# Padding a selector to 128 columns, moving three blocks of work in time, and changing an eviction ratio in a one-core training-step kernel

## The chip, the cores and the metric

The kernel runs on one core of one Trainium2 chip. The metric is device microseconds (us) of one execution; a "median" is that of several executions, and the "span" is that of the one execution that was profiled. All runs quoted here are of the fast state, that is, none shows the longer time at a lower clock that some executions have. Engine names in the profile: PE is TensorE (matmuls), PEld its weight loads, DVE VectorE, ACT ScalarE, POOL GpSimd, SP SyncE. An "eviction" here is a copy of a finished PSUM tile to SBUF.

## The reference

The kernel computes a transformer block with adaptive layernorm and the gradient of all its inputs. S = 2048, D = 512, 32 heads of 16, F = 1792, bf16. What matters of the forward part:

```python
def _A_ref(x, wqkv, wo):            # H = 32, Dh = 16, W = 8, dil = 2
    qkv = (x @ wqkv) ...            # -> q, k, v
    idx = pos[:, None] - off[None, :]          # off = 0, 2, .., 14
    logits = einsum('bhsd,bhswd->bhsw', q, kg) * scale   # 8 shifted keys a query
    attn = softmax(where(mask, logits, -1e9))
    return (einsum('bhsw,bhswd->bhsd', attn, vg)) ... @ wo

h = layernorm(x) * (1 + ca) + sa
x = x + ga * _A_ref(h, A_wqkv, A_wo)
h = layernorm(x) * (1 + cb) + sb
x = x + gb * ((h @ w_gate) * (h @ w_up)) @ w_down
# (sa, ca, ga, sb, cb, gb) = silu(c) @ w_mod
# the result is x and the gradients of 8 inputs for a given grad_out
```

## The kernel before

It is one long program of stages; a library places waits and hands out buffers from pools. Each pool tile is named by a tag, and a tag has a fixed number of buffers. Five places matter.

Logits: q times a shifted k on VectorE, then a 64-column selector matmul on TensorE sums over each head's 16 rows. The projection matmuls of the next head tile come between.

```python
Gsel = const.tile([P, W, 8 * W], BF16, name="Gsel")        # 64 columns
psA, psB, psT: PSUM pools of 2, 4 and 2 buffers

def logits_ht(ht):
    htpair, htlo = divmod(ht, 2)
    for sc in range(NCH):
        lt_ps = ps_tile(psA, "lt_ps")
        for w in range(W):
            prod = wt(0, "prodL")
            ew.mul(prod[:], qT[...], kT[... shifted by DIL * w ...])
            nc.tensor.matmul(lt_ps[htlo * 64:(htlo + 1) * 64, :], lhsT=Gsel[:, w, :], rhs=prod[:], start=(w == 0), stop=(w == W - 1))
        evac(LT_sb[htlo * 64:...], lt_ps[htlo * 64:...])
for ht in range(DC):
    qkv_proj(0 * DC + ht); qkv_proj(1 * DC + ht)     # q and k
    if ht >= 1: logits_ht(ht - 1)
for ht in range(DC):
    qkv_proj(2 * DC + ht)                            # v
    if ht == 0: logits_ht(DC - 1)
# ... softmax; attn_tok is carved from the big buffer tag BIG1, as W1 and h1T are
```

FFN output: 56 transposes of Wd (its copy is stored for the backward part) stand ahead of the matmuls.

```python
for fc in range(FC):                                 # FC = 14
    for dc in range(DC):
        nc.tensor.transpose(out=stgw[:, dc, :], in_=Wd[:, fc, ...], identity=ident[:])
    evac(wTt[:], stgw[:], eng="v"); store(WdT_d[...], wTt[:])
```

Attention backward, "the accumulation stage", 128 steps (4 head tiles x 4 chunks x 8 shifts):

```python
evac.set_ratio(3, 1)       # of each 4 evictions, 3 on ScalarE and the 4th on VectorE
for w in range(W):
    nc.tensor.matmul(arep_ps[:], lhsT=RepSel[...], rhs=attnT2[...])     # 2 buffers for
    evac(arep_sb[:], arep_ps[:])                                        # arep and
    nc.tensor.matmul(dlrep_ps[:], lhsT=RepSel[...], rhs=dlT[...])       # dlrep together
    evac(dlrep_sb[:], dlrep_ps[:])
    ew.mul(Y, arep_sb, d_oT);    shifted_acc(dv_ps, ..., Y, w)          # VectorE, TensorE
    ew.mul(Pq, dlrep_sb, kT2);   nc.tensor.matmul(dq_ps[:], lhsT=ident, rhs=Pq)
    ew.mul(Pk, dlrep_sb, qT2);   shifted_acc(dk_ps, ..., Pk, w)         # Pk: tag wb4
```

The end: the weight gradient dwqkv (48 steps of 4 transposes, an eviction and 4 matmuls), then 16 tiles of layernorm backward, then the gradient of c.

```python
for fq in range(3):
    for t in range(NT):
        ... 4 transposes, evac(stg_sb, stg, eng="v"), 4 matmuls into dwq_acc
for t in range(NT):
    x_l = wt(4, "x_l9");  load(x_l[:], x_dram[:, t, :])        # tag wb4
    ... 12 matmuls dh1_ps, then ln_bwd_tile: n_bwd (ACT), dn (DVE, ACT), qq (DVE, ACT),
        negm, Aq (DVE), Bq (ACT), dx (DVE), prodca (DVE), dca_ps (PE)
for n in (0, 1): dwmod_chunk(n)
for dc in range(DC):                       # 4 multiply-reduces of 3072 columns
    nc.vector.tensor_tensor_reduce(out=junk10, in0=wmod2[:, dc, :], in1=dmod_rep, ...)
nc.sync.dma_start(out=out_7.rearrange("o (dc p) -> p (o dc)", p=P), in_=dc_bf[:])   # 1 KB
```

## Time and profile before

| | before |
|---|---|
| median of 15 runs | 1367.41 us (1365.33 to 1371.49) |
| profiled span | 1366.9 us |
| granted TensorE clock, mean | 0.921 |
| busy share PE / DVE / ACT | 82 / 62 / 37% |

The page's first two parts: busy time of each engine, then the busy tenths in 40 equal slices of the span (here the rows of three engines and of the granted clock).

```profile
span 1366.9 us, 16522 instructions
PE 1118.5 (82%) x5743; PEld 508.6 (37%) x5828; DVE 851.5 (62%) x2291; ACT 501.2 (37%) x939; POOL 117.3 (9%) x226
...
PE   3799499759989788979997888869768888899860
...
DVE  6567799984446654763444223234979999954465
ACT  2333467513321111454445010012036666643471
...
PEclk9699699869999899989997999989889999999985
```

No engine binds the whole. The rows must be read slice by slice (34 us each): PE is at 9 in slices 3 and 4 (the logits), DVE at 9 from slice 31 to 35 (the accumulation stage), and in the last slice PE is at 0.

The view of windows shows the same by stage: window, its length, then busy us of each engine with the number of instructions, then granted clock, DMA share and GB/s.

```profile
core 0: us, PE busy (x) PEld busy (x) DVE busy (x) ACT busy (x) POOL busy (x), PEclk, DMA share, GB/s
57.00:141.00 84.00, 82.89 (x292) 25.98 (x296) 50.43 (x128) 33.63 (x59) 1.06 (x2) 0.99 0.12 51
141.00:170.00 29.00, 10.45 (x67) 5.94 (x68) 25.58 (x81) 11.74 (x23) 1.06 (x2) 0.54 0.27 105
397.00:467.00 70.00, 60.57 (x308) 27.73 (x312) 43.93 (x120) 8.37 (x17) 19.36 (x32) 0.98 0.37 115
1019.00:1209.00 190.00, 166.39 (x813) 68.95 (x813) 178.99 (x463) 122.99 (x222) 0.00 (x0) 0.99 0.05 10
1209.00:1367.00 158.00, 108.98 (x600) 51.32 (x610) 75.34 (x180) 64.33 (x135) 12.85 (x21) 0.87 0.24 86
```

Logits: PE is busy 82.9 of 84 us. But busy is not the same as fast: the timeline of PE (start, duration, line, operation) has three consecutive starts there.

```profile
86.04 0.40 PE L359 MATMUL lt_ps<-prodL,Gsel 128*64 128x512 bf16 x1
86.38 0.39 PE L345 MATMUL qkv_ps<-big_p 128*128 128x512 bf16 x1
86.70 0.40 PE L359 MATMUL lt_ps<-prodL,Gsel 128*64 128x512 bf16 x1
```

The starts are 0.34 and 0.32 us apart where the weight is 64 columns wide in one matmul and 128 in the next. Between two projection matmuls they are about 0.22 apart, between two selectors 0.24. The timeline of the weight loads (PEld) shows what is lost: at each change of width the load starts together with its own matmul (86.04 and 86.38, as above), after the matmul before it has been issued.

```profile
86.04 0.11 PEld L359 LDWEIGHTS <-Gsel 128*64 128x64 bf16 x1 [0.23 <-issue]
86.38 0.10 PEld L345 LDWEIGHTS <-big_p 128*128 128x128 bf16 x1 [0.23 <-issue]
```

So it is, within about 5 ns, at all but one of the 167 changes of width between the first and the last logits matmul; between neighbours of one width the load mostly starts 0.21 us ahead or more, under the matmul before.

The accumulation stage: VectorE is busy 179 of 190 us, and the view of groups shows what it does beside multiplying (busy us, mean ns of one, then idle time before it). A ScalarE eviction of the same tile is a little shorter, 598 against 681 ns.

```profile
L62 DVE CAST dlrep_sb<-dlrep_ps 128x512 bf16<-128x512 f32 x64 | 43.6, 681 | 0.2 <-PE dlrep_ps L803 0.2
L60 ACT ACTIVATE dlrep_sb<-dlrep_ps 128x512 bf16<-128x512 f32 x64 | 38.3, 598 | 29.0 <-PE dlrep_ps L803 26.2 <-DVE Pq L84 1.4 <-DVE Yv L84 0.9
```

The end: the timeline has the last of four multiply-reduces and then a small store; the view of DMA issues gives the store's size and the us from issue to landing.

```profile
1347.88 3.36 DVE L888 CUSTOM_DVE_ANT_0 m_p<-big_p,m_p 128x3072 bf16<-128x3072 bf16 x1
...
1351.68 0.39 SPq L899 DMA_DIRECT2D out_dram<-dc_bf  x1
```
```profile
out_dram<-dc_bf SPq DMA_DIRECT2D x1, 1.0 KB, 14.1
```

The kernel ends when one kilobyte has landed, 14.1 us after it was issued, with every engine idle.

### The profile page before, as it was taken

How to read it: one execution, taken by the hardware profiler on the slowest of the kernel's cores; microseconds unless marked ns; L12 is line 12 of the kernel's file. 1: busy time of each engine (PE TensorE's matmuls, PEld its weight loads, DVE VectorE, ACT ScalarE, POOL GpSimd, SP SyncE). 2: the span in 40 equal slices, each digit the busy share in tenths (PEclk: the TensorE clock that was granted, in tenths of full speed). 3: DMA queues.
4: the chain of work that ended last, by engine and by line, in shares of the span. 5: the costliest groups of instructions: out<-in, count | busy, mean ns of one | idle time of the engine just before them, and what ended most of it. 6: DMA issues, size and time to landing. Idle time of an engine off the chain costs nothing. (4 is left out here: it accounts for less than half of the span.)

```text
span 1366.9 us, 16522 instructions
## 1 busy us (share of the span) xinstructions
PE 1118.5 (82%) x5743; PEld 508.6 (37%) x5828; DVE 851.5 (62%) x2291; ACT 501.2 (37%) x939; POOL 117.3 (9%) x226
## 2 busy tenths in 40 slices
PE   3799499759989788979997888869768888899860
PEld 1332233324444244434442455444233333345420
DVE  6567799984446654763444223234979999954465
ACT  2333467513321111454445010012036666643471
POOL 2000000221122311001111000000000000000010
PEclk9699699869999899989997999989889999999985
DMA  6111200542243420122323005050101000041121
GB/s 215 47 63 63 100 9 1 218 129 75 65 127 97 153 78 28 51 104 82 97 85 140 34 31 211 16 162 4 43 17 31 1 1 0 1 177 58 62 67 38
DMA packets 62691, 101.94 MB, mean 75 GB/s; under 512 B 29712, under 2 KB 50448, under 8 KB 60560
## 3 DMA queue, kind: packets, MB, share of 16 engines
q1 hardware_dynamic: 50400, 56.21, 12.7%
q0 software_dynamic: 12208, 44.67, 8.8%
q8 instruction: 45, 0.74, 0.2%
q14 instruction: 38, 0.31, 0.1%
HBM read 54.10 MB, written 44.66 MB: 72 GB/s over the span
## 5 line engine op out<-in xcount | busy, mean ns | idle before, releaser
L62 DVE COPY stg_sb<-stg 128x512 bf16<-128x512 bf16 (+1 forms) x248 | 90.0, 401 | 209.7 <-PE stg L666 102.4
L671 PE MATMUL dw_acc<-stg_sb,m_h2tok 128*128 128x512 bf16 (+1 forms) x497 | 108.4, 356 | 20.7 <-DVE stg_sb L62 17.9
L60 ACT ACTIVATE arep_sb<-arep_ps 128x512 bf16<-128x512 f32 x128 | 76.5, 597 | 33.1 <-PE arep_ps L799 32.8
L671 PEld LDWEIGHTS <-m_h2tok 128*128 128x128 bf16 x512 | 49.6, 98 | 68.6 <-issue 27.1
L84 DVE TENSOR_TENSOR prodL<-big_qkv 128x512 bf16<-128x512 bf16 x128 | 50.4, 423 | 36.3 <-PE lt_ps L359 29.8
L62 DVE CAST big_u<-gu_ps 128x512 bf16<-128x512 f32 x56 | 38.7, 691 | 51.3 <-PE gu_ps L477 51.3
L550 PE MATMUL dwd_ps<-m_dffn,stg_sb 128*128 128x512 bf16 x215 | 54.1, 390 | 14.8 <-DVE stg_sb L62 14.2
L803 PE MATMUL dlrep_ps<-m_p,RepSel 128*128 128x512 bf16 x128 | 48.7, 381 | 19.0 <-ACT dlrep_sb L60 10.6
L60 ACT ACTIVATE dw_sb<-dw_acc 128x512 bf16<-128x512 f32 (+1 forms) x32 | 14.8, 550 | 133.5 <-issue 116.3
L345 PE MATMUL qkv_ps<-big_p 128*128 128x512 bf16 x184 | 60.0, 414 | 3.4 <-DVE big_p L62 1.9
L627 PE MATMUL dh_ps<-m_wgT,big_u 128*128 128x512 bf16 x218 | 55.4, 393 | 7.3 <-DMA m_wgT<-WgT_d 6.9
L60 ACT ACTIVATE big_g<-gu_ps 128x512 bf16<-128x512 f32 x56 | 33.4, 597 | 74.7 <-PE gu_ps L477 74.7
L477 PE MATMUL gu_ps<-m_h2T,wgb 128*128 128x512 bf16 x219 | 58.1, 386 | 0.9 <-DVE rstd L293 0.8
L84 DVE TENSOR_TENSOR Yv<-arep_sb,big_p 128x512 bf16<-128x512 bf16 x128 | 52.9, 413 | 8.4 <-ACT arep_sb L60 8.4
L477 PE MATMUL gu_ps<-m_h2T,wub 128*128 128x512 bf16 x218 | 57.6, 383 | 0.5 <-issue 0.2
L84 DVE TENSOR_TENSOR Pq<-dlrep_sb,big_qkv 128x512 bf16<-128x512 bf16 x128 | 53.4, 417 | 2.8 <-ACT dlrep_sb L60 1.4
L629 PE MATMUL dh_ps<-m_wuT,big_g 128*128 128x512 bf16 x220 | 54.8, 379 | 0.2
L422 PE MATMUL rep_ps<-big_p,RepSel 128*128 128x512 bf16 x127 | 48.9, 386 | 6.1 <-ACT rep_sb L60 1.6
L60 ACT ACTIVATE rep_sb<-rep_ps 128x512 bf16<-128x512 f32 x86 | 46.9, 596 | 19.0 <-PE rep_ps L422 19.0
L512 PE MATMUL ffn_acc<-m_wd,hh 128*128 128x512 bf16 x218 | 53.0, 386 | 0.9 <-DVE hh L84 0.8
L84 DVE TENSOR_TENSOR Pk<-dlrep_sb,big_qkv 128x512 bf16<-128x512 bf16 x128 | 53.1, 415 | 0.0
L799 PE MATMUL arep_ps<-m_p,RepSel 128*128 128x512 bf16 x127 | 48.4, 381 | 4.6 <-ACT dlrep_sb L60 2.7
(233 smaller groups left out, 2240.9 us busy)
## 6 DMA issues: line engine op xcount, KB each, us to landing
qkvT_d<-big_qkv POOLq DMA_DIRECT2D x3, 2080.0 KB, 6.6
big_qkv<-qkvT_d SPq DMA_DIRECT2D x3, 2080.0 KB, 13.1
big_p<-in_w_mod_dram SPq DMA_DIRECT2D x2, 3072.0 KB, 12.5
x_l<-x_d SPq DMA_DIRECT2D x32, 128.0 KB, 2.1
out_dram<-dwm_sb POOLq DMA_DIRECT2D x6, 512.0 KB, 3.4
out_dram<-dw_sb POOLq DMA_DIRECT2D x6, 512.0 KB, 3.3
m_x<-in_A_x_dram SPq DMA_DIRECT2D x4, 512.0 KB, 11.0
h_d<-m_h POOLq DMA_DIRECT2D x4, 512.0 KB, 3.0
```

Of the source, the lines that this page charges most:

```text
L60: nc.scalar.activation(out=out, in_=in_, func=ACT.Copy)
L62: nc.vector.tensor_copy(out=out, in_=in_)
L84: self.eng(force).tensor_tensor(out=out, in0=in0, in1=in1, op=op)
L345: nc.tensor.matmul(ps[:], lhsT=W1[:, dc, ft * P:(ft + 1) * P], rhs=h1T[:, dc, sc * 512:(sc + 1) * 512], start=(dc == 0), stop=(dc == DC - 1))
L422: nc.tensor.matmul(rep_ps[:], lhsT=RepSel[:, htlo, w, :], rhs=attnT[:, htpair, sc * 512:(sc + 1) * 512], start=True, stop=True)
L477: nc.tensor.matmul(ps[:], lhsT=Wb[:, dc, :], rhs=h2T[:, dc, sc * 512:(sc + 1) * 512], start=(dc == 0), stop=(dc == DC - 1))
L512: nc.tensor.matmul(accs[tt][:], lhsT=hh[:, tt * P:(tt + 1) * P], rhs=Wd[:, ft, :], start=(ft == 0), stop=(ft == FC - 1))
L550: nc.tensor.matmul(dwd_ps[:], lhsT=stg_sb[:, tt, :], rhs=d_ffn_tok[:, t, :], start=(t == 0), stop=(t == NT - 1))
L627: nc.tensor.matmul(dh2_ps[:], lhsT=DGT[:, fc, t * P:(t + 1) * P], rhs=WgT[:, fc, :], start=(fc == 0), stop=False)
L629: nc.tensor.matmul(dh2_ps[:], lhsT=DUT[:, fc, t * P:(t + 1) * P], rhs=WuT[:, fc, :], start=False, stop=(fc == FC - 1))
L671: nc.tensor.matmul(accs[dt][:, 0:fw], lhsT=h2_tok[:, t, dt * P:(dt + 1) * P], rhs=rhs, start=(t == 0), stop=(t == NT - 1))
L803: nc.tensor.matmul(dlrep_ps[:], lhsT=RepSel[:, htlo, w, :], rhs=dlT[:, htpair, s0:s0 + 512], start=True, stop=True)
```

## The change

Its intent: take the width switching out of the logits; fill TensorE where it idles (V projection under the softmax, Wd transposes under the first layernorm); take evictions off VectorE in the accumulation stage; and put the small serial work of the end under the dwqkv matmuls. The diff, cut to its core (two unused scratch tensors are also declared; two head tiles now share one PSUM tile for the logits and one eviction, for which the PSUM pools of logits and projection are exchanged):

```diff
+    GselP = const.tile([P, 2, W, P], BF16, name="GselP")      # 128 columns, half of them zero
 ...
+    Wd_e = _carve(big1, DC * S + 3 * DC * D, [FC, D])
+    load(Wd_e, B_w_down.rearrange("(fc p) d -> p fc d", p=P))
     for t in range(NT):                                       # layernorm 1
         ...
+        if t >= 2:                                            # one fc of Wd a tile
+            ... 4 transposes, evac(wTd[:], stgw[:], eng="s"), store(WdT_d[...])
 ...
-            ps = ps_tile(psB, "qkv_ps")
+            ps = ps_tile(psA, "qkv_ps")
 ...
-                nc.tensor.matmul(lt_ps[htlo * 64:(htlo + 1) * 64, :], lhsT=Gsel[:, w, :], rhs=prod[:], start=(w == 0), stop=(w == W - 1))
+                nc.tensor.matmul(lt_ps[:], lhsT=GselP[:, htlo, w, :], rhs=prod[:], start=(htlo == 0 and w == 0), stop=(htlo == 1 and w == W - 1))
 ...
-    for ht in range(DC):
-        qkv_proj(2 * DC + ht)
-        if ht == 0:
-            logits_ht(DC - 1)
+    logits_ht(DC - 1)
     ...                                                       # softmax of 16 tiles
+    for ht in range(DC):
+        qkv_proj(2 * DC + ht)
 ...
-    for fc in range(FC):  ... the transposes of Wd in the FFN stage ...
 ...
-                        nc.tensor.matmul(ps[htlo * 64:(htlo + 1) * 64, :], lhsT=Gsel[:, w, :], ...)   # dA stage
+                        nc.tensor.matmul(ps[:], lhsT=GselP[:, htlo, w, :], ...)
 ...
-    evac.set_ratio(3, 1)
+    evac.set_ratio(15, 1)
 ...
-    load(h1_tok2, h1_d[:]); load(wmod2, ...)
-    for fq in range(3):   ... dwqkv, ahead of the layernorm backward ...
     for t in range(NT):                                       # layernorm backward
         ...
+        if t == 3:
+            load(h1_tok2, h1_d[:]); load(wmod2, ...)
     for n in (0, 1):
-        dwmod_chunk(n)
+        dwmod_chunk(n, end=True)
+    ... dwqkv here, the transposes of the next step ahead of the matmuls of this one ...
     for dc in range(DC):
-        nc.vector.tensor_tensor_reduce(out=junk10, in0=wmod2[:, dc, :], ...)
+        for n in range(6):                                    # six pieces of 512 columns
+            nc.vector.tensor_tensor_reduce(out=junk10[:, 0:D], ...)
```

## The prediction

> **What bounds it now.** No single engine (page: TensorE 82%, VectorE 62%, ScalarE 37% of 1366.9 us); busy times by stretch show stages with different limits.
>
> - 57-141 us (Q/K/V projection and logits): TensorE busy 83 of 84 us. The timeline shows matmul starts 0.216 us apart while the output width stays at 128, but about 0.33 us apart wherever a 64-wide selector matmul alternates with a 128-wide projection matmul (0.24 between selectors). Some 167 switches x ~0.11 make about 19 us. Weight loads take 107 ns for the selector, 97 otherwise. The Trainium skill (TensorE: Matmul & The Clock Gate, Weight-path perf modes) says fast weight load needs 128 weight columns; the trace agrees in direction.
> - 141-170 (softmax): VectorE busy 25.6 of 29, TensorE 10.5.
> - 397-467 (FFN output): TensorE, with 56 transposes of Wd in between.
> - 1019-1209 (attention backward accumulation): VectorE busy 179 of 190. Starts are 0.335 us apart for its multiplies, 0.60 for its evictions of PSUM; ScalarE evictions start 0.494 apart.
> - 1209-1367 (end): 16 layernorm-backward tiles at 4.23 us each, bound by a ScalarE/VectorE chain; then four 3.36 us multiply-reduces; then a 1 KB store that takes 14.1 us to land, all in series.
>
> **What the change does.**
>
> 1. Selector padded to 128 columns: same matmul count, switching gone. V projection moved to fill TensorE later (instruction order: half among the last logits, half in softmax). Logits then become VectorE-bound (128 x 0.335 = 43 us plus gaps of two blocks of 20 projection matmuls, 4.4 us each). Against that: Wd's load lands only near 39 us, and 56 transposes with ScalarE evictions crowd layernorm 1, which ends about 5 us later; the V evictions hold up some exponentials, about 3 us. First output-stage matmul: 168 -> about 151 us. **-17 us.**
> 2. The 56 Wd transposes leave the FFN stage: their starts take about 5 us and the waits around them about 6. **-9 us.**
> 3. Padded selector in the dA stage: only its first part is TensorE-bound; the rest stays VectorE-bound. **-2 us.**
> 4. Eviction ratio 15:1 removes 48 of 64 VectorE evictions (48 x 0.60 = 29 us). Per 8 steps VectorE then needs 24 x 0.335 + 2 x 0.60 = 9.2 us, ScalarE 15 x 0.494 + 2 x 0.48 = 8.4, TensorE about 9.0: balanced, so the two-deep chain matmul 0.38, evict 0.60, multiply 0.41 through in-order TensorE limits, about 1.25 us a step plus the accumulator hand-overs. 190 -> 166 us. **-24 us.**
> 5. End: layernorm backward first (16 x 4.23 + 3 = 71 us, little TensorE filling until its last three tiles), then the dwqkv matmuls (48 steps x 1.09 us, about 9 hidden), under which the reduces and the 14.1 us store now hide. Then evictions and a 512 KB store, 7 us. 158 -> 123 us. **-35 us.**
>
> All five lie on the path. Sum -87: **1280 us**, range 1255 to 1308. Faster by over 2%: 0.95; within 2%: 0.04; slower: 0.01.
>
> **Signs.** Matmul spacing about 0.22 in logits; logits' multiplies back to back; no transposes in the FFN; VectorE no longer near 94% in the backward stage, no engine alone above 95%; the last thing in the chain is the dwqkv store, not the small one.
>
> **What would make it wrong.** Layernorm 1 stalling on Wd longer than 5 us; the backward stage held near 180 us by the two eviction buffers; input tiles queued behind the 5 MB load at the end.

## The result, and the profile after

| | before | after |
|---|---|---|
| median | 1367.41 us | 1296.39 us (1295.82 to 1298.61, 8 runs) |
| ratio of the fast runs | 1 | 0.948, 95% interval 0.9468 to 0.9491 |
| profiled span | 1366.9 us | 1294.5 us |
| granted TensorE clock, mean | 0.921 | 0.944 |

A ratio is the mean time of one kernel's fast runs over that of the other's fast runs of the same rounds, so it is not quite the ratio of the medians that stand beside it. Where experiments are compared with each other, their ratios to the kernel before are used, since chips and rounds differ by some tenths of a per cent (the kernel before had medians from 1367 to 1370 us in the four sets of rounds).

The prediction of 1280 (1255 to 1308) holds, but the time is 16 us above its centre. The lead over the kernel before, read from matmul starts in the two traces, shows where it is won (us from the start of the span; the accumulation stage is counted here and below from the first of the 64 transposes that stand before its steps to the last dq matmul):

| event | before | after | lead | won in this part | predicted |
|---|---|---|---|---|---|
| last transpose of layernorm 1 | 52.0 | 53.6 | -1.6 | -1.6 | -5 |
| first logits matmul | 66.8 | 65.6 | 1.2 | 2.8 | |
| last logits matmul | 141.4 | 115.3 | 26.2 | 25.0 | |
| first matmul of the attention output | 168.3 | 147.7 | 20.6 | -5.6 | 17 up to here |
| first FFN output matmul | 397.6 | 377.9 | 19.7 | -0.9 | |
| first matmul of dWd | 473.0 | 443.4 | 29.6 | 9.9 | 9 |
| first matmul of dO | 914.4 | 884.7 | 29.7 | 0.1 | |
| start of the accumulation stage | 1010.8 | 980.8 | 30.0 | 0.3 | 2 |
| last dq matmul | 1209.1 | 1161.9 | 47.2 | 17.2 | 24 |
| end | 1366.9 | 1294.5 | 72.4 | 25.2 | 35 |

The same parts of the page:

```profile
span 1294.5 us, 16642 instructions
PE 1090.8 (84%) x5743; PEld 508.3 (39%) x5828; DVE 821.7 (63%) x2286; ACT 530.5 (41%) x993; POOL 118.9 (9%) x227
...
PE   2798599669999688979998888877976999998797
...
DVE  6578899974456654773445123222796999984693
ACT  2544477423321011453444201112105888886731
...
PEclk9899699779999899999998799998987999999999
```

The same stages in the view of windows:

```profile
57.00:115.00 58.00, 57.73 (x256) 24.93 (x260) 43.03 (x128) 23.66 (x40) 1.09 (x2) 1.00 0.20 80
115.00:148.00 33.00, 16.68 (x94) 8.27 (x95) 25.83 (x82) 16.12 (x31) 1.06 (x2) 0.75 0.20 81
378.00:437.00 59.00, 54.44 (x245) 23.61 (x247) 38.71 (x105) 8.26 (x16) 9.16 (x17) 1.00 0.32 104
990.00:1162.00 172.00, 162.88 (x808) 67.58 (x808) 156.51 (x414) 148.10 (x269) 0.00 (x0) 0.99 0.05 10
1162.00:1294.00 132.00, 108.85 (x605) 51.65 (x614) 77.78 (x223) 64.30 (x135) 12.45 (x21) 0.99 0.33 104
```

The first line is still bound mainly by TensorE: the prediction had VectorE as the next limit there, and it is busy 43 of 58. That TensorE is busy 57.7 of 58 would not prove it, as busy is not fast; but from the first to the last logits matmul some 217 starts at 0.216 us would take 47 of the 49.6 us. Only part of the spacings between two selectors, up to 0.335 us, are the pace of VectorE's multiplies. In the accumulation stage all three engines are now near each other (163, 157 and 148 of 172).

The timeline of PE in the logits now has even starts, 0.21 and 0.22 us apart:

```profile
85.68 0.38 PE L382 MATMUL lt_ps<-prodL,GselP 128*128 128x512 bf16 x1
85.89 0.38 PE L364 MATMUL qkv_ps<-big_p 128*128 128x512 bf16 x1
86.11 0.62 PE L382 MATMUL lt_ps<-prodL,GselP 128*128 128x512 bf16 x2
```

The evictions of the accumulation stage, in the view of groups, with 48 moved to ScalarE:

```profile
L62 DVE CAST dlrep_sb<-dlrep_ps 128x512 bf16<-128x512 f32 x16 | 10.9, 684 | 0.0
L60 ACT ACTIVATE dlrep_sb<-dlrep_ps 128x512 bf16<-128x512 f32 x112 | 67.2, 600 | 8.6 <-PE dlrep_ps L823 3.3 <-DVE Yv L84 0.6 <-PE arep_ps L819 0.5
```

Two new waits appear. In the view of waits between 115 and 148 us (who, for whom, us in total, times, longest), VectorE's write of the attention waits for a V projection matmul. And at the start of the end part the timeline of ScalarE has a normalisation waiting for its input tile.

```profile
DVE big_p L423 <- PE qkv_ps L364: 5.0, 1, 5.0
```
```profile
1169.85 0.81 ACT L616 ACTIVATE n_bwd<-x_l,nmr,rstd 128x512 bf16<-128x512 bf16 x1 [3.68 <-DMA x_l<-in_A_x_dram]
```

The kernel now ends as the intent had it, with the last dwqkv evictions and their store (timeline); the small store is issued at 1265.3 and is hidden.

```profile
1286.62 2.06 ACT L60 ACTIVATE dwq_sb<-dwq_acc 128x512 bf16<-128x512 f32 x4 [17.25 <-issue]
1288.97 0.75 POOL L147 DMA_DIRECT2D out_dram<-dwq_sb  x1 [18.57 <-ACT dwq_sb L60]
```

### The profile page after: what moved, and what is told of

Same layout as the page of the kernel before. It is cut to its first block, busy times and chain, and to the rows that moved or that the text cites. A ratio compares the mean times of both kernels' runs of the same rounds, so it can differ in the third digit from the quotient of the medians.

```text
span 1294.5 us, 16642 instructions
## 1 busy us (share of the span) xinstructions
PE 1090.8 (84%) x5743; PEld 508.3 (39%) x5828; DVE 821.7 (63%) x2286; ACT 530.5 (41%) x993; POOL 118.9 (9%) x227
## 5 line engine op out<-in xcount | busy, mean ns | idle before, releaser
L60 ACT ACTIVATE arep_sb<-arep_ps 128x512 bf16<-128x512 f32 x128 | 76.6, 598 | 13.7 <-PE arep_ps L819 8.9
L60 ACT ACTIVATE dlrep_sb<-dlrep_ps 128x512 bf16<-128x512 f32 x112 | 67.2, 600 | 8.6 <-PE dlrep_ps L823 3.3
L84 DVE TENSOR_TENSOR Yv<-arep_sb,big_p 128x512 bf16<-128x512 bf16 x128 | 53.5, 418 | 10.9 <-ACT arep_sb L60 10.8
L84 DVE TENSOR_TENSOR prodL<-big_qkv 128x512 bf16<-128x512 bf16 x128 | 43.3, 416 | 17.6 <-PE lt_ps L382 15.0
L84 DVE TENSOR_TENSOR prodO<-rep_sb,big_qkv 128x512 bf16<-128x512 bf16 x128 | 48.3, 419 | 5.6 <-ACT rep_sb L60 5.5
L364 PE MATMUL qkv_ps<-big_p 128*128 128x512 bf16 x183 | 50.3, 383 | 1.8 <-ACT big_qkv L60 1.4
```

The lines of the kernel that those rows point to most:

```text
L60: nc.scalar.activation(out=out, in_=in_, func=ACT.Copy)
L84: self.eng(force).tensor_tensor(out=out, in0=in0, in1=in1, op=op)
L364: nc.tensor.matmul(ps[:], lhsT=W1[:, dc, ft * P:(ft + 1) * P], rhs=h1T[:, dc, sc * 512:(sc + 1) * 512], start=(dc == 0), stop=(dc == DC - 1))
```

## The experiments

All twelve gave correct results. The first five add one part of the change to the kernel before; the others edit the kernel after.

### e_width: only the width, only in the logits

The first question is whether the 20.6 us of the front come from the width or from the V projection's new place.

```diff
+    GselP = ...                                              # as in the change
-                nc.tensor.matmul(lt_ps[htlo * 64:(htlo + 1) * 64, :], lhsT=Gsel[:, w, :], rhs=prod[:], ...)
+                nc.tensor.matmul(lt_ps[:], lhsT=GselP[:, htlo, w, :], rhs=prod[:], ...)
```

> The kernel before with one thing changed: the logits selector is 128 columns wide (zeros in the other half, half of the result rows used); V projection, Wd transposes, ratio and end stay as before. Theory A (switching between 64-wide and 128-wide matmuls costs about 0.11 us each time): matmul starts in the logits become 0.216 us apart on every kind of neighbour, the logits turn VectorE-bound, and 36 V matmuls are left between logits and softmax; first output-stage matmul moves from 168 to about 155 us, time -13 us (-11 to -16), about 1354. Theory B (the 20.6 us that the change won before the output stage come from running the V projection under the softmax, and width is minor): less than 4 us gained.

Measured: 1349.91 us median, 17.5 below the kernel before, ratio 0.987 (0.9846 to 0.9893). The last logits matmul starts at 114.5 us and the first output matmul at 149.1, 19.2 us before that of the kernel before; 2.3 of these are there before the first logits matmul (64.5 against 66.8), for a reason that was not looked into. The timeline of PE, and of one weight load:

```profile
84.14 0.38 PE L351 MATMUL qkv_ps<-big_p 128*128 128x512 bf16 x1
84.35 0.60 PE L365 MATMUL lt_ps<-prodL,GselP 128*128 128x512 bf16 x2
84.58 0.10 PEld L351 LDWEIGHTS <-big_p 128*128 128x128 bf16 x1
84.79 0.38 PE L351 MATMUL qkv_ps<-big_p 128*128 128x512 bf16 x1
```

Zero columns were added, so the array does more useless work, and yet the stage is faster: starts of 0.21 to 0.22 us replace 0.32 to 0.34. Nearly the whole gain of the front is the width, more than theory A expected. The weight load (84.58) now mostly starts 0.21 us ahead of its matmul (84.79) between the two kinds as well. A load of the narrow selector is only 11 ns longer than one of 128 columns (107 against 96), so it is the lost overlap that costs, and not the slower load. The edit changes the columns of the weight and the rows of the result at once; which of them keeps the load from starting early was not separated.

### e_vmove: only the V projection's place

```diff
-    for ht in range(DC):
-        qkv_proj(2 * DC + ht)
-        if ht == 0:
-            logits_ht(DC - 1)
+    logits_ht(DC - 1)
     ... softmax ...
+    for ht in range(DC):
+        qkv_proj(2 * DC + ht)
```

> The kernel before with the V projection alone moved behind the softmax in program order; the selector stays 64 wide. Theory A: the scheduler still interleaves the V matmuls one by one with the narrow selector matmuls, each costing two switches, so the logits stay TensorE-bound: 0 to -3 us. Theory B (overlap with softmax is what pays): -12 to -16 us.

Measured: 1366.98 us, ratio 1.0003 (0.9973 to 1.0033); first output matmul at 168.6 us (168.3 before). The move alone is worth nothing, but it also moved nothing: the trace has no V matmul after the last logits matmul (the last projection matmul starts at 142.1, the last of the logits at 142.5), as theory A said. So this run does not test what an overlap with the softmax pays. The wide selector is what leaves V matmuls over: 36 projection matmuls come after the last logits matmul in e_width, 38 are recorded there in the kernel after. From e_width to the kernel after, where they no longer stand ahead of the softmax in program order, the first output matmul comes only 1.4 us earlier (149.1 to 147.7); a_attn, below, shows what held it up.

### e_wd: only the transposes of Wd

```diff
+        if t >= 2:
+            ... 4 transposes of Wd_e, eviction on ScalarE, store ...   # layernorm 1
-    for fc in range(FC): ... the same in the FFN stage ...
```

> The kernel before with only the 56 Wd transposes, their evictions (now ScalarE) and stores moved into layernorm 1. Theory A: the FFN output stage loses them, first FFN matmul to last closing matmul goes from 69 to about 59 us, and layernorm 1 absorbs them in TensorE idle time: -9 to -10.5 us. Theory B (layernorm 1 pays part back, since Wd lands only near 39 us and the first projection matmul waits for it): -4 to -7 us, with the first logits matmul later than 66.8 us.

Measured: 1360.11 us, ratio 0.994 (0.9916 to 0.9964). The FFN output stage, first matmul to the last of dgb, falls from 68.8 to 58.9 us, and the first logits matmul is at 66.5 us (66.8 before): the transposes cost nothing where they went. The median fell by 7.3 us, between the two theories; the profiled run by 9.8. The first projection matmul starts at 38.5 instead of 31.1 us, because it waits behind the first transposes of Wd, which wait for its load until 36.4, but the layernorm had not been waiting for it.

### e_ratio: only the eviction ratio

```diff
-    evac.set_ratio(3, 1)
+    evac.set_ratio(15, 1)
```

> The kernel before with only the eviction ratio of the attention backward accumulation set to 15:1. If the stages are independent: the same -17 us as that stage won in the change (188.9 to about 172 us from first to last matmul), VectorE waiting in small pieces. If the stage's gain in the change came partly from elsewhere (other clock, other placement): clearly less, under -13 us.

Measured: 1351.23 us, ratio 0.9879 (0.9859 to 0.99). The accumulation stage takes 181.4 us, as in the kernel after (181.1), against 198.3 before.

### e_end: only the end

```diff
-    ... dwqkv, then layernorm backward, then reduces, then the small store ...
+    ... layernorm backward, then dwqkv with the reduces and the small store under it ...
```

> The kernel before with only the last stage of the change (layernorm backward first, pipelined dwqkv, reduces split in six). If independent of the rest: the -25 us that the stage won in the change (from the last accumulation matmul to the end 157.8 -> about 132.6). Rival: part of the win needs the other edits; then under -20.

Measured: 1341.26 us, ratio 0.9796 (0.9781 to 0.981). From the last dq matmul to the end it takes 130.4 us (157.8 before, 132.6 in the kernel after).

The differences of the single parts' medians to the kernel before of their own rounds are -17.5 (width), -0.4 (V), -7.3 (Wd), -16.1 (ratio) and -27.9 (end), together about -69, against -71.0 for the whole change. The intervals of the single ratios are 2 to 4 us wide to each side, about 7 for the sum (an estimate: root of the sum of squares). Within this noise the parts add up, so the larger part of the missing 16 us was not lost to one part disturbing another. (The selector of the dA stage and the shared PSUM tile of the logits were not run alone.) What was missed is to be looked for inside the parts, above all the two that fell short, the accumulation stage and the end.

### a_allact and a_seven: how far the ratio carries

Both are the kernel after with another ratio.

```diff
-    evac.set_ratio(15, 1)
+    evac.set_ratio(1, 0)       # a_allact: all on ScalarE
+    evac.set_ratio(7, 1)       # a_seven
```

> The changed kernel with all evictions of the backward accumulation on ScalarE (none of 16 left on VectorE). Theory A (the stage is now held by the in-order chain matmul, evict, multiply; ScalarE issues evictions 0.494 us apart, so 256 + 32 of them need 142 of 171 us, and each VectorE eviction makes one step 1.73 instead of about 1.2 us): stage shorter by 5 to 8 us against the changed kernel, total about 1290. Theory B (ScalarE, 94% busy there by summed durations, is the new bound): 16 more evictions make it longer by 6 to 8 us, about 1304.

> The changed kernel with the ratio 7:1 (32 evictions on VectorE instead of 16). Theory A (chain; VectorE evictions make long steps): 5 to 8 us slower than the changed kernel, about 1303. Theory B (ScalarE bound): 5 to 8 us faster, about 1290.

Measured: a_allact 1292.78 us, ratio 0.9442 (0.9429 to 0.9455), stage 177.0 us; a_seven 1300.84 us, ratio 0.9501 (0.9488 to 0.9514), stage 183.9 us. With the two known ones:

| ratio | VectorE evictions of 256 | stage, us | us per eviction taken off, from the row above |
|---|---|---|---|
| 3:1 | 64 | 198.3 | |
| 7:1 | 32 | 183.9 | 0.45 |
| 15:1 | 16 | 181.1 | 0.18 |
| all ScalarE | 0 | 177.0 | 0.26 |

The view of windows of a_allact in the stage:

```profile
985.00:1158.00 173.00, 161.63 (x840) 67.96 (x838) 149.97 (x398) 161.75 (x291) 0.00 (x0) 0.99 0.05 10
```

Here ScalarE is busy 161.8 of 173 us and TensorE 161.6. Both runs go the way of theory A and against B, so ScalarE was not the limit; both steps, 4.1 and 2.8 us of the stage, are smaller than the 5 to 8 that A expected. The first 32 evictions taken off VectorE paid 0.45 us each; the rest paid about half of that. This fits a pace set by the chain matmul, eviction, multiply, matmul, and in the kernel after the waits are spread along it: TensorE's weight loads waited 11.6 us for Pk, VectorE 9.0 for evictions of dlrep, ScalarE 8.9 for arep matmuls. But the chain is argued and not isolated: the two PSUM buffers that arep and dlrep share, which the prediction named as a risk, were never varied. In the kernel after, the starts of the dq matmuls of one group of eight shifts are 1.71, 1.13, 1.31, 1.55, 1.27, 1.16, 1.73 and 1.04 us apart: the 1.73 stands at the one VectorE eviction of the group (all 16 such steps take 1.60 to 1.73), and 1.71 follows the evictions of the last group's accumulators; at 1.55 ScalarE had waited 0.47 us for a VectorE product. The mean of this group is 1.36; over all 127 spacings it is 1.34 and the median 1.27. In a_allact the median is 1.25.

### a_swap: the waiting input tile

The wait of 3.7 us for x_l may come from the queue of the loads, or from its buffer: x_l has tag wb4, whose buffers the products Pk of the accumulation stage hold to the last. The experiment swaps the tags of two inputs, so that x_l takes buffers that the stage does not use.

```diff
-        x_l = wt(4, "x_l9")
+        x_l = wt(5, "x_l9")
-        dx1_l = wt(5, "dx1_l9")
+        dx1_l = wt(4, "dx1_l9")
```

> The changed kernel with the two input buffers of the last layernorm backward exchanged, so that x comes into buffers that the accumulation stage does not use and can be loaded early. Theory A (the first normalisation waits 3.7 us for x, whose buffers are still held by the accumulation stage): -3 to -4 us against the changed kernel. Theory B (the wait is due to the 5 MB load in the same queue and would come anyway, on the other input): 0 to -1 us.

Measured: 1295.42 us, ratio 0.9456 (0.9443 to 0.9469). The wait is gone. From the last dq matmul to the last dca matmul it takes 73.8 us (76.6 in the kernel after). So the held buffer was needed for the wait. But the queue had its part: in the kernel after, SyncE issues the load of x_l, once the buffer is free, 0.42 us behind the 2 MB load of h1 (the x4 are the loads of four tiles),

```profile
1161.60 0.32 SPq L150 DMA_DIRECT2D big_p<-h_d  x1
1162.02 2.22 SPq L150 DMA_DIRECT2D x_l<-in_A_x_dram  x4
```

and the slowest of these x_l loads takes 7.7 us to land, where their median is 2.4. In a_swap dx1_l takes this place behind the load of h1; its slowest load takes 10.2 us, but only 0.5 us of waiting for it is seen. The total can't settle the 2.8 us: the ratios differ by 3.3 us (0.9456 against 0.948, intervals just overlapping), the medians by 1.0.

### a_attn: what V under the softmax holds up

The prediction counted 3 us for this and named the exponentials. The trace names a buffer: attn_tok is carved from the next tile of tag BIG1, whose old tile V's matmuls still read, so the first attention tile can be written only after the last V matmul. The experiment carves attn_tok from the free half of the logits tile.

```diff
-    attn_tok = _carve(big1, 4 * S + DC * S + DC * D, [NT, H * W])
+    attn_tok = _carve(m2, 2 * S, [NT, H * W])
```

> The kernel after, with the attention tile moved out of the large shared buffer into the free half of the logits buffer, so that its first write no longer has to wait for the last V projection matmul. Theory (V under the softmax delays it through that buffer): the 5.0 us wait of VectorE for the projection goes, the stretch from the last logits matmul to the first output-stage matmul falls from 32.5 to about 28 us, the total by about 4 us (1296 to about 1292). Rival (the softmax is bound by the work of VectorE and of the ScalarE evictions of V): the wait moves to another engine, the stretch falls by under 2 us and the total by under 2.

Measured: 1297.35 us, ratio 0.9471 (0.9457 to 0.9484). The wait is gone from the view of waits, and from the last logits matmul to the first output matmul it takes 27.3 us (32.5 in the kernel after, 26.9 before). The total gained about 1 us by the ratios (0.9471 against 0.948, within the noise), where the theory had 4. Part of the 5 us is still there at the last dq matmul (1158.9 against 1161.9), but nothing at the end (1295.8 against 1294.5). The last lines of PE show where they go:

```profile
1274.18 0.39 PE L889 MATMUL stg<-ident,big_qkv 128*128 128x128 bf16 x4
1278.35 1.50 PE L904 MATMUL dwq_acc<-stg_sb,big_p 128*128 128x512 bf16 x4 [3.79 <-DVE stg_sb L62]
...
1280.07 1.91 PE L904 MATMUL dwq_acc<-stg_sb,big_p 128*128 128x512 bf16 x4
```

TensorE waits 3.79 us for an eviction that VectorE could not start for 5.0 us; the profile names no releaser of the core for it ("remote"). The kernel after has a short form of the same stop at the same step (2.9 us between steps instead of 1.09). After it four matmuls take 1.50 and 1.91 us instead of 1.03, and the granted clock is 0.84 and 0.73 in the two stretches of 4 us from 1276 on, where the kernel after has 1.00. The Trainium skill (TensorE: Matmul & The Clock Gate, "What's actually happening") says that an idle window of about 3.4 us halves the array's clock until it has been busy again; the granted clock is 0.50 in the 3.4 us from 1278.75 on, and the starts there are about 0.43 us apart instead of 0.216, which agrees. So the theory of the buffer is shown for its own stage, and the total did not follow for a reason that lies elsewhere. What makes the eviction late is open.

### a_fill: dwqkv steps among the layernorm tiles

```diff
+        if t >= 4:
+            dwq_step()         # at the end of each layernorm-backward tile: one of the 48 steps
```

> The kernel after, with one step of the dwqkv matmuls put after each layernorm-backward tile from the fifth on (12 of 48 steps). Theory (matmuls that stand behind the layernorm chain in program order are hidden only at its end, about 4 to 5 steps of them): 12 hidden steps instead, the tiles keep their 4.2 us, and the end from the last dq matmul falls from 132.6 to about 124 us, total about 1288. Rival (the steps share VectorE and the PSUM buffers with the layernorm chain, so each costs the chain what it saves): tiles of 4.7 us or more and a total within 3 us of 1296.

Measured: 1294.58 us, ratio 0.9445 (0.9428 to 0.9462). The premise of this expectation was miscounted. In the kernel after, 8 steps (32 matmuls of 192) stand before the last dca matmul, not 4 to 5; here it is 16 (64 matmuls). The tiles take 4.37 us instead of 4.23, and from the last dq matmul to the end it takes 128.1 us instead of 132.6. So 8 more hidden steps, 8.7 us of work by the 1.09 us of a step, brought 4.5 (4.8 in the total, by the ratios). The timelines of ScalarE and PE show what took the rest:

```profile
1250.06 1.09 ACT L60 ACTIVATE dwq_sb<-dwq_acc 128x512 bf16<-128x512 f32 x2 [0.84 <-DMA out_dram<-dwm_sb]
```
```profile
1250.70 1.86 PE L880 MATMUL dwq_acc<-stg_sb,big_p 128*128 128x512 bf16 x4 [2.12 <-ACT dwq_sb L60]
```

The first group of 16 steps is now done at 1239.1 us. Its four accumulators are evicted by ScalarE, which has in front of them, in order, the last layernorm tile and the eight evictions of dwmod, and which then waits for a store to give its buffer back. No dwqkv matmul starts for 11.6 us, and the granted clock in the 21 us after 1245 is 0.76.

### a_pipe: the next normalisation ahead of the last activation

```diff
     ... Aq on VectorE ...
+    between()                  # n_bwd of tile t + 1
     nc.scalar.activation(out=Bq[:], in_=Aq[:], ...)
```

> The kernel after, with the normalisation of the next tile issued on ScalarE ahead of the last activation of the present tile. Theory (the 4.23 us of a tile is an in-order chain in which ScalarE stands idle 1.0 us a tile waiting for VectorE): the gap is filled, the tile takes about 3.5 us, 16 tiles save about 10 us, of which some 2 are lost because less of the dwqkv work hides; total about 1288. Rival (the chain through VectorE and TensorE sets the tile's time whatever ScalarE's order): 4.1 us or more, total within 3 us of 1296.

Measured: 1302.56 us, ratio 0.9505 (0.9492 to 0.9519), slower than the kernel after. Neither theory was tested, because the edit did not do what it was meant to do. The timeline of ScalarE:

```profile
1218.24 0.81 ACT L635 ACTIVATE Bq<-Aq,nb,rstd 128x512 bf16<-128x512 bf16 x1 [1.01 <-DVE Aq L631]
1218.96 0.80 ACT L865 ACTIVATE n_bwd<-x_l,nmr,rstd 128x512 bf16<-128x512 bf16 x1
```

The normalisation was written ahead of Bq and runs behind it, so the gap of 1.01 us before Bq stays. It now stands between Bq and the next tile's work, and a tile takes 4.35 us instead of 4.23. Its 0.80 us agree with the Trainium skill (ScalarE: Activation LUTs, "What ACT_TABLE_LOAD costs"): 186 ns + 0.833 ns a column, and 93 ns for each of two pointer operands, give an estimate of 799 ns. The first normalisation also waits longer for its input, 6.24 us instead of 3.68: it now stands on ScalarE ahead of the first tile's other work (the eviction dh_bf and dn), which the kernel after does in the meantime. Its load was issued 0.4 us after that of h1, as there. Whether filling the gap would shorten a tile stays open.

### a_best: five edits together

The edits of a_allact, a_swap, a_attn, a_fill and a_pipe in one kernel.

> The kernel after with five edits together: all evictions of the accumulation stage on ScalarE (-3.6 us when alone), the input buffers of the last layernorm swapped (-1), the attention tile moved (-4), the dwqkv steps spread under the layernorm tiles (-8) and the next normalisation issued early (-8). If they add up: about 1272 us, ratio to the kernel before about 0.930. If spreading and early normalisation compete for the same idle time, about 1280.

Measured: 1281.47 us (1280.44 to 1283.77), ratio 0.9355 (0.9342 to 0.9368): the fastest of all, about 17 us below the kernel after by the ratios (0.9355 against 0.948; 15 by the medians). In its trace the softmax stretch has lost 5.2 us (115.2 to 142.5, 27.3 us), the accumulation stage takes 176.1 instead of 181.1, and the end 124.6 instead of 132.6. That is not the full expectation of 1272: the spreading leaves an 8.4 us hole between two dwqkv groups, and a tile still takes 4.35 us. A version without a_pipe's edit was not run.

## Why the prediction was right, and where it was off

**Step 1, front (-17 predicted, -20.6 measured): right mechanism, two terms mis-sized.** Taking the switching away was put at 19 us; e_width shows 17.5 in the medians, and in its trace 19.2, of which 2.3 arose before the logits. The term "layernorm 1 ends about 5 us later" was too large: it ends 1.6 us later, and e_wd shows that the first logits matmul is not delayed at all. "Logits then become VectorE-bound" was wrong: TensorE's starts alone account for about 47 of the 49.6 us from first to last logits matmul, and the sign "multiplies back to back" did not come true (VectorE is busy 43 of 58 us). "V evictions hold up some exponentials, about 3 us" was wrong in its cause and too small: the softmax stretch grew by 5.6 us, of which 5.2 vanish when the attention tile no longer waits for V's matmuls through the shared buffer (a_attn). Moving V, which the prediction took as a part of the gain, moves nothing by itself (e_vmove), and on top of the wide selector it brought 1.4 us before the buffer was freed. That these errors partly cancel is luck.

**Step 2, FFN (-9 predicted, -9.9 measured): right.** e_wd gives the same 9.9 for the stage alone (7.3 in the medians of the whole kernel).

**Step 3, dA stage (-2 predicted, -0.3 measured): too large.** The selector there is as wide as in the logits, but the stretch is 96.4 us before and 96.1 after. No experiment was made for so small a term.

**Step 4, accumulation (-24 predicted, -17.2 measured): right mechanism, mis-sized term.** From the first to the last dq matmul the stage takes 187.8 us before (the prediction had taken 190) and 170.8 after, where 166 was predicted. Most of the steps are as predicted: "about 1.25 us a step" stands against a median of 1.27. The term that failed is what was added for the exceptions, 6 us (166 less 128 x 1.25) for "accumulator hand-overs" alone: the 16 evictions left on VectorE were counted as VectorE's work (2 x 0.60 in eight steps) and not as a delay of the chain, where each makes a step of up to 1.73 us. Without them the same stretch takes 166.8 us (a_allact). The prediction's own sum had all three engines at 8.4 to 9.2 us per eight steps and called that balanced; the group of eight shown ran at 10.9.

**Step 5, end (-35 predicted, -25.2 measured): right mechanism, mis-sized terms.** It was 71 for the layernorm, 7 for the tail and so 45 for the rest of dwqkv, 123 (39 steps of 1.09 would be 42.5). Measured: 76.6, 48.3 and 7.7. Of the 5.6 us in the layernorm, 2.8 go with the wait for x_l (a_swap), and about 1.2 are the last three tiles, which end 4.94, 4.34 and 4.63 us apart instead of 4.23 while dwqkv transposes and the first dwmod evictions run on the same engines; the rest lies in the first tile. "Input tiles queued behind the 5 MB load" was foreseen in the prediction's last paragraph, and it came true for the 2 MB of it that were issued just ahead of x_l; that a held buffer would put x_l behind them was not foreseen. The number of hidden steps was nearly right (8 against 9). The remaining 40 steps took 1.21 us each instead of 1.09, because the dwmod matmuls and one stop of 1.8 us lie among them.

Between the traces the lead is 72.4 us where the prediction had 87. Of these 14.6 us, 6.8 lie in step 4, 9.8 in step 5 and 1.7 in step 3; the front and the FFN gave 4.5 back, and 0.8 were lost between the stages.

## What to carry to other kernels

A busy engine is not a fast one: read the starts, and where two matmul shapes alternate, compare their spacing with that of one shape alone, and see whether the weight loads still start ahead; the cure may pay even if it adds useless columns. A stage in which three engines are "balanced" by their busy sums can run slower than the largest of them, here by about 18% (10.9 against 9.2 us per eight steps), so an estimate should add the steps that are not like the others. When work is moved in time, look in the trace whether it ran elsewhere at all (e_vmove), and list the buffers that it reads and writes: both new waits here came from shared pool tags, and a wait that is removed early can be eaten by a stop at the end.

## What the Trainium skill lacked or had wrong

- TensorE: Matmul & The Clock Gate, "Weight-path perf modes" and Part 3, and TensorEngine Tiling (Array Packing), "Key Properties": the first says when fast weight load is on, the last that a change of tiling mode drains TensorE, but no page gives the cost of alternating between 64 and 128 weight columns. Here starts were 0.32 to 0.34 us apart when alternating, 0.24 between 64-wide ones and about 0.22 between 128-wide ones, because at a change the weight load of about 0.1 us did not start ahead; padding with zeros saved 17.5 us (e_width).
- TensorE: Matmul & The Clock Gate, "Back-to-back issue gap": it gives 216 ns for an isolated gap at N = 512, which these traces show, and about 131 ns as sustained spacing in a stream of weight load and matmul. The streams read here, 84 us and 58 us of nearly unbroken matmuls among them, do not go below 0.21 us.
- DMA: Bandwidth & Descriptors, "Anatomy of one DMA" puts the fixed cost at about 2.0 us (fitted for another issuing path). The 1 KB store of 512 scattered two-byte elements took 14.1 us from issue to landing, and 128 KB input tiles 2.1 us. The page has no figure for so small and scattered a store.
- No page says what the stop of VectorE was that the profile calls "remote" (5.0 us in a_attn, in the same step shorter in the kernel after). It stays open.
